# Threshold attention and an ELU layer on one core: two kinds of TensorE stretches of a pair joined, the tails' turned squares moved

## The chip, the cores and the metric

One core of a Trainium2 chip runs the kernel. The metric is the device time of one execution in microseconds (us), the median of several runs. TensorE is called PE, VectorE DVE, ScalarE ACT, GpSimd POOL; SP (SyncE) issues nearly all transfers.

## The reference

```python
# q, k, v: (8, 8, 576, 64) fp32; tau 0.02; w_in (512, 2048); w_out (2048, 512)
scores = scale * np.matmul(q, k.transpose(0, 1, 3, 2))
thresh = np.max(scores, axis=-1, keepdims=True) - tau
scores = np.where(scores >= thresh, scores, -1000000000.0)
scores = scores - np.max(scores, axis=-1, keepdims=True)
attn = np.exp(scores)
attn = attn / (np.sum(attn, axis=-1, keepdims=True) + 1e-09)
attn_out = np.matmul(attn, v)
x = attn_out.transpose(0, 2, 1, 3).reshape(8 * 576, 512)
h = x @ w_in
g = np.where(h > 0.0, h, np.exp(np.minimum(h, 0.0)) - 1.0)
out = g @ w_out
```

Per head, 576 queries meet 576 keys; a weight is kept where the score lies within tau of the row's maximum. The heads' outputs, put side by side, go through two dense layers with an ELU between. All of it is fp32.

## The kernel before, in words

**Work.** Heads are taken two at a time: 32 pairs (8 batches of 4 pairs). A head's 576 rows are four blocks of 128 (blocks 0 to 3) and a tail of 64; the two tails of a pair make block 4. Scores have the head's 64 dimensions as contraction, so they use 64 of the array's 128 rows: the two heads lie in the two row halves, and the output is cut into column halves of 64 too (tile form 64\*64, four quarters at once). Every other matmul contracts over 128 rows and is cut into column halves alone (128\*64).

**A step of the steady stage** (line numbers of the kernel before; pairs START = 9 to 31, the loop near line 1798) puts on PE, for pair p:
- `tail_step` (1725), which calls `tails_and_values` (829): scores of pair p's tails (line 852) and, beside them in the other quarters, the tails' part of the values of pair p − 2 (857), all 64\*64; then the main part of those values in 128\*64 (865, part 1 of 320 columns, then part 0 of 256);
- `wide_step` (1741) half 0: scores of blocks 0 and 1 (`wide_scores`, 785, matmuls on line 802);
- `ffn_quarters` (1692): 14 quarters of the dense layers' products (line 772, through `by_columns`). The products are Strassen-like (seven products for eight); they are fed by sums of blocks of x (`sums_x`, 1086), which are made once in four pairs;
- half 1: scores of blocks 2 and 3, and 14 more quarters.

**After the scores.** For each block and head: maximum (DVE, 809), bound (POOL, 818), exponential (ACT, 822), mask with sum (DVE, 826), then reciprocal (560) and scaling (POOL, 503). The weights of a block are turned with `turn_squares` (644): DVE transposes 32x32 squares into a buffer `x` of the pool `squares` (two buffers), SP sends it to DRAM in four transfers (683), and `fetch` (689) brings it back into its place in `wTa` (blocks 0 and 1) or `wTb` (blocks 2 and 3, three to four squares wide, with block 4's square fetched to the edges of both). These are what the values of the pair read in `tail_step` two steps later.

**PSUM.** Eight banks of 512 fp32 columns: five are the tile `sc` (the wide scores, and in its banks 1 to 4 values and the tails' scores), three are f0, f1, f2, which the products take in turn.

**What sets the order.** An agenda (`at`, 1432; `on_pe`, 1449) sorts all instructions by due times, which advance with PE's planned costs. `MOVED` shifts the due time of a named instruction in odd steps ("f...") or even steps ("s..."), `FIRST` in one step; names are like turn2 (the transposes of block 2) or fetch3. Each engine runs its own queue in that order and waits only for semaphores. SP's queue is in order too: a fetch that waits for its send holds what is behind it. The early stage (pairs 0 to 8) follows a hand-written list, `EARLY`. `on_banks` (744) adds the waits among engines bank by bank for the tile `sc`, in place of waits for the whole tile.

Of the kernel before, what the change touches and what calls it, by code (L numbers as in the profile page):

```python
# [20 lines left out]
    "9:3.0": 0.61, "9:fetch0": -3.6, "9:turn4": 2.44, "e:139.1": 0.46, "e:140.2": -0.49, "e:176.2": 1.07,  # L21
    "e:203p0": 1.03, "e:30.2": 0.35, "e:73p0": 1.88, "e:75p0": 1.3, "e:77.2": -1.81, "e:78.1": -3.94, "e:9b":
    -2.29, "e:e30": -0.75,
# [140 lines left out]
half.61 bsend.8.0 bmax.8.3.0 bmax.8.3.1 bmax.8.2.1 bth.8.3 half.58 bnorm.8.1.1 bmax.8.2.0 v.8 chg.7.0 bturn.8.1  # L164
bexp.8.2.0 bth.8.2 half.59 chg.1.1 bexp.8.2.1 scale.9 bexp.8.3.0 landed.7.4 bmask.8.2.1 fin.1.0 bmask.8.2.0 half.62
bsend.8.1 bexp.8.3.1 bsu.8.2 bmask.8.3.0 brec.8.2 half.63 bmask.8.3.1 bnorm.8.2.1 bnorm.8.2.0:act load.k.10 bsu.8.3
brec.8.3 bturn.8.2 bnorm.8.3.1 fin.1.1 bnorm.8.3.0 store.0.0 bturn.8.3 store.1.0 store.1.1 bsend.8.2 bsend.8.3
# [9 lines left out]
def kernel(  # L177
# [10 lines left out]
    nc = tc.nc  # L188
# [35 lines left out]
    granted, banks_at_start = [None], {x: psum["f"].tile([P, 512], FP32, name=x) for x in ("f0", "f1", "f2")}  # L224
# [233 lines left out]
    wTs, xts, open_steps, turns = {}, {}, {}, {}  # L458
# [230 lines left out]
    def fetch(pr, i, queue=nc.sync):  # L689
        back = turns.pop((pr, i)).rearrange("c k p n -> (c k) p n")  # L690
        wT, g0 = turned_tile(pr, i)
# [52 lines left out]
    def on_banks(made, ap, kept=True):  # L744

        ins, needed, starts = made.ins, [], [ap.offset % (5 * 512)]
# [19 lines left out]
        tc.add_to_no_dep_group(engine, ins)  # L766

    def by_columns(o, left, right, note=None, **how):
        n = o.shape[0]
        for y in range(0, n, D):  # L770
            oy = o[y : y + D] if n > D else o
            made = nc.tensor.matmul(oy, left[:, y : y + D] if n > D else left, right, skip_group_check=True, **how)  # L772
            if note:
                note(made, oy)

    def watch(made, ap):
        if ap.tensor.name == wide[0].tensor.name:
            on_banks(made, ap)
# [6 lines left out]
    def wide_scores(pr, half, parts=(0, 1)):  # L785

        qT, kT, _ = pairs[pr]
        for s in range(2) if parts[0] == 0 else ():
            i = 2 * half + s
            st = open_step(pr, i, turned_by[1 - s])  # L790
# [3 lines left out]
        order = (((0, 0, 0, 448), (1, 1, 0, 320), (1, 1, 320, 256), (0, 0, 448, 128)),  # L794
                 ((1, 0, 0, 256), (0, 1, 0, 384), (1, 0, 256, 320), (0, 1, 384, 192)))
        for h, s, c, n in [x for part in parts for x in order[part]]:
# [7 lines left out]
            if (h, s, c) == (1, 1, 0):  # L804
                on_banks(nc.scalar.copy(seen, o[:, :1]), o[:, :1], kept=False)

    def wide_max(pr, i, h):
        st = open_steps[pr, i]
        on_banks(nc.vector.tensor_reduce(st["mx"][:, h : h + 1], st["sc", h], axis=AX.XY if i == NC else AX.X, op=ALU.max,  # L809
# [19 lines left out]
    def tails_and_values(pr, before):  # L829

        pv, sc = (wide[0].rearrange("p (x n) -> p x n", n=512)[:, b : b + 2] for b in (1, 3))
# [15 lines left out]
        for a in range(2):  # L847
            for h in range(2):
# [5 lines left out]
                if before is not None:  # L854
                    g0, g1 = span(h, x)
                    o = pv[r, x, g0 * T : g1 * T]
# [1311 lines left out]
```

## Time and profile before

| | us |
|---|---|
| median of three runs | 1256.89 |
| lowest, highest | 1255.64, 1258.02 |
| profiled execution | 1254.87 |
| its span, first to last instruction | 1253.1 |
| DVE, POOL, ACT busy | 1067.1, 790.8, 585.1 |

The page of the profile gives the busy time of each engine, the granted clock, the chain of work that ended last, and groups of instructions by line. The views used beside it are the waits (who waited for whom), the timeline (instructions in order of time, merged by line) and windows (busy time of each engine in a stretch). A length of a matmul in the timeline has a modelled end; starts are recorded. A pair's step is about 33.9 us long.

### The profile page before, as it was taken

How to read it: one execution, taken by the hardware profiler on the slowest of the kernel's cores; microseconds unless marked ns; L12 is line 12 of the kernel's file. 1: busy time of each engine (PE TensorE's matmuls, PEld its weight loads, DVE VectorE, ACT ScalarE, POOL GpSimd, SP SyncE). 2: the span in 40 equal slices, each digit the busy share in tenths (PEclk: the TensorE clock that was granted, in tenths of full speed). 3: DMA queues.
4: the chain of work that ended last, by engine and by line, in shares of the span. 5: the costliest groups of instructions: out<-in, count | busy, mean ns of one | idle time of the engine just before them, and what ended most of it. 6: DMA issues, size and time to landing. Idle time of an engine off the chain costs nothing.

```text
span 1253.1 us, 32264 instructions
## 1 busy us (share of the span) xinstructions
PE 1238.7 (99%) x11999; PEld 826.4 (66%) x11999; DVE 1067.1 (85%) x2322; ACT 585.1 (47%) x1276; POOL 790.8 (63%) x1147
## 2 busy tenths in 40 slices
PE   8999999999999999999999999999999999999998
PEld 5776576466666666666666666666666666678887
DVE  6998989898889889898889888988989885777877
ACT  7987755453534445352625353444535260434130
POOL 5775545686576747674767657675767473675564
PEclk9999999999999999999999999999999999999999
DMA  8568899998989898899889898989889876444433
GB/s 226 151 181 240 231 256 262 251 293 222 267 204 261 230 244 223 260 251 244 236 228 269 224 261 211 266 222 249 215 258 251 238 217 223 163 139 153 137 112 116
DMA packets 332940, 278.31 MB, mean 222 GB/s; under 512 B 201328, under 2 KB 288368, under 8 KB 332784
## 3 DMA queue, kind: packets, MB, share of 16 engines
q1 hardware_dynamic: 331264, 275.57, 79.2%
q8 instruction: 94, 1.54, 0.5%
q10 hardware_dynamic: 1520, 0.69, 0.2%
q14 instruction: 62, 0.51, 0.1%
HBM read 178.85 MB, written 97.32 MB: 220 GB/s over the span
## 4 chain that ended last, share of the span: by engine, by line
PE 84%; DVE 1%; DMA 0%; issue 0%; ACT 0%; POOL 0%; SPq 0%; DVEq 0%; ACTq 0%; POOLq 0%
PE f L772 61%; PE sc L865 9%; PE sc L802 9%; PE f L992 2%; PE sc L857 1%; PE f L924 1%; PE sc L852 1%; DMA wTb<-there 0%; DVE mx L809 0%; DVE x L649 0%; DVE w_one L826 0%; DVE e L826 0%; DVE x L662 0%; DVE g L938 0%; ACT w_one L426 0%
## 5 line engine op out<-in xcount | busy, mean ns | idle before, releaser
L809 DVE TENSOR_REDUCE mx<-sc 128x1 f32<-128x576 f32 x252 | 180.1, 746 | 33.0 <-PE sc L802 28.6
L822 ACT ACTIVATE w_one<-sc,mx 128x576 f32<-128x576 f32 x140 | 100.9, 741 | 131.9 <-DVE mx L809 110.7
L818 POOL TENSOR_SCALAR th<-mx,ntau 128x2 f32<-128x2 f32 (+1 forms) x140 | 45.9, 329 | 183.1 <-DVE mx L809 183.0
L826 DVE SCALAR_TENSOR_TENSOR w_one<-sc,th,w_one 128x576 f32<-128x576 f32 x140 | 110.0, 813 | 20.3 <-ACT w_one L822 19.0
L772 PE MATMUL f<-xt,sw 128*64 128x256 f32 x1024 | 123.2, 382 | 0.6 <-ACT xt L432 0.5
L802 PE MATMUL sc<-kT,qT 64*64 64x320 f32 (+5 forms) x1792 | 122.2, 409 | 1.3 <-DVE su L554 0.5
L772 PE MATMUL f<-x,w_in_sb 128*64 128x256 f32 x1024 | 123.0, 380 | 0.0
L822 ACT ACTIVATE e<-sc,mx 128x576 f32<-128x576 f32 x112 | 82.9, 743 | 85.6 <-DVE mx L809 84.2
L772 PE MATMUL f<-xt,w_in_sb 128*64 128x256 f32 x1024 | 121.8, 379 | 0.5 <-DVE xt L1092 0.5
L503 POOL TENSOR_SCALAR w_one<-w_one,rs 128x576 f32<-128x576 f32 x115 | 89.4, 787 | 38.8 <-DVE rs L560 38.8
L649 DVE STREAM_TRANSPOSE x<-w_one 128x512 f32<-128x512 f32 (+1 forms) x140 | 100.0, 744 | 14.7 <-POOL w_one L503 9.6
L802 PEld LDWEIGHTS sc<-kT,qT 64*64 64x64 f32 x1792 | 81.1, 132 | 45.6 <-issue 18.5
L772 PE MATMUL f<-w_out_sb,s 128*64 128x256 f32 (+1 forms) x896 | 105.6, 376 | 0.0
L772 PE MATMUL f<-w_out_sb,g 128*64 128x256 f32 (+1 forms) x864 | 101.7, 376 | 0.0
L772 PEld LDWEIGHTS f<-x,w_in_sb 128*64 128x64 f32 x1024 | 74.4, 137 | 37.5 <-ACT g L1547 4.4
L772 PEld LDWEIGHTS f<-xt,w_in_sb 128*64 128x64 f32 x1024 | 75.4, 137 | 35.8 <-ACT e L822 0.9
L772 PEld LDWEIGHTS f<-xt,sw 128*64 128x64 f32 x1024 | 71.8, 137 | 40.9 <-issue 5.5
L826 DVE SCALAR_TENSOR_TENSOR e<-sc,th,e 128x576 f32<-128x576 f32 x112 | 87.8, 808 | 7.8 <-ACT e L822 7.4
L772 PE MATMUL f<-t,s 128*64 128x256 f32 (+1 forms) x800 | 93.5, 375 | 0.0
L772 PEld LDWEIGHTS f<-w_out_sb,s 128*64 128x64 f32 x896 | 63.7, 137 | 31.5 <-issue 3.2
L772 PEld LDWEIGHTS f<-w_out_sb,g 128*64 128x64 f32 x864 | 61.2, 137 | 31.7 <-issue 3.7
L649 DVE STREAM_TRANSPOSE x<-e 128x640 f32<-128x640 f32 x108 | 77.5, 756 | 3.6 <-POOL e L429 0.8
(324 smaller groups left out, 2800.5 us busy)
## 6 DMA issues: line engine op xcount, KB each, us to landing
there<-x SPq DMA_DIRECT2D x452, 144.0 KB, 3.9
wTb<-there SPq DMA_DIRECT2D x58, 576.0 KB, 6.5
wTa<-there SPq DMA_DIRECT2D x55, 576.0 KB, 4.9
sw<-win_sums SPq DMA_DIRECT2D x62, 384.0 KB, 4.1
t<-wout_sums SPq DMA_DIRECT2D x45, 512.0 KB, 5.3
there<-x SPq DMA_DIRECT2D x112, 80.0 KB, 1.9
wTb<-there SPq DMA_DIRECT2D x56, 160.0 KB, 3.7
wst<-in_moe_w_in_dram SPq DMA_DIRECT2D x16, 512.0 KB, 5.2
```

Of the source, the lines that this page charges most:

```text
L503: nc.gpsimd.tensor_scalar(wv, wv, st["rs"][:, h : h + 1], 1.0, ALU.mult, ALU.mult)
L649: nc.vector.transpose(x[:, :, c0 : c0 + nc_], src.rearrange("p (c g n) -> p g c n", c=nc_, n=T))
L772: made = nc.tensor.matmul(oy, left[:, y : y + D] if n > D else left, right, skip_group_check=True, **how)
L802: on_banks(nc.tensor.matmul(oy, qT[r, i * P + y * D : i * P + (y + 1) * D], kT[r, k0 : k0 + n], start=True, stop=True, skip_group_check=Tr ...
L809: on_banks(nc.vector.tensor_reduce(st["mx"][:, h : h + 1], st["sc", h], axis=AX.XY if i == NC else AX.X, op=ALU.max, negate=True), st["sc" ...
L818: nc.gpsimd.tensor_scalar(st["th"][:, cs], st["mx"][:, cs], -1.0, ntau, ALU.mult, ALU.add)
L822: on_banks(nc.scalar.activation(st["e", h], st["sc", h], AF.Exp, bias=st["mx"][:, h : h + 1]), st["sc", h])
L826: on_banks(nc.vector.scalar_tensor_tensor(st["e", h], st["sc", h], st["th"][:, h : h + 1], st["e", h], ALU.is_ge, ALU.mult, accum_out=st[" ...
L852: on_banks(nc.tensor.matmul(o, qT[r, MAIN:], kT[r, TAIL + x * HALF : TAIL + (x + 1) * HALF], start=True, stop=True, skip_group_check=True), o)
L857: on_banks(nc.tensor.matmul(o, vd[r, r], parts[x][r, g0:g1, NC], start=True, stop=False, skip_group_check=True), o)
L865: on_banks(nc.tensor.matmul(o, vm[:, h, c], parts[part][:, g0:g1, h * (NC + 1) + c], start=False, stop=(c == NC - 1), skip_group_check=Tru ...
L992: nc.tensor.matmul(cur[c, i][:, :DM], hidden(c, ft % NU, 1)[:, 0, ft // NU, i], w_out_sb[:, ft], start=(ft == 0), stop=(ft == NFT - 1))
```

## The change

The order of PE's work in a step is changed. `wide_step(pr - 1, 1)`, the scores of blocks 2 and 3 of the pair before, now stands directly ahead of `tail_step(pr)`, and the first 14 quarters directly behind the values; then come the scores of blocks 0 and 1 and the other 14 quarters. The tail step of the steady stage is the new `tails_apart`: the tails' scores lie behind the four wide ones, in the last columns of a tile `sc` that has six banks (f0 is its sixth), and the values lie in the product banks f2 (part 1) and f1 (part 0). After a tail step the products' banks come in the order f2, f0, f1.

With scores of blocks 2, 3 and 4 in hand at once there are three squares to turn; block 4's is now turned into the place in `wTb` that belongs to block 3 of the pair before and isn't fetched yet. The input sums are made in halves: the first half a pair earlier (for the first group in the early stage, on POOL by the list), the second around the tail step. Helpers tell the framework that groups of instructions use different banks. The due times, `FIRST` and `MOVED` are new for nearly all names. In the last stage six banks instead of five come from the closed tile, and the weights' sums of step 32 follow the last transposes.

```diff
@@ tables of due times (cut; two of the names that are spoken of)
-    1.44, "sturn1": 0.3, "sturn2": -0.07, "sturn3": 0.1, "sturn4": -3.1, "sx0": -0.87, "sx1": -0.05, "sx10":
+    7.54, "ssum4": 1.62, "sturn0": 2.13, "sturn1": 4.55, "sturn2": 7.64, "sturn3": 6.15, "sturn4": 5.52, "sw8": 0.32,
+    "fturn1": 4.12, "fturn2": 5.56, "fturn3": 5.24, "fturn4": 3.76, "fx0": 0.22, "fx1": -0.22, "fx10": 2.53, "fx11":
@@ PSUM
-    wide = [psum["w"].tile([P, 5 * 512], FP32, name="sc")]
-    banks_at_start["t"] = wide[0][:, 4 * 512 :]
+    wide = [psum["w"].tile([P, 6 * 512], FP32, name="sc")]
+    banks_at_start["f0"] = wide[0][:, 5 * 512 :]
+    banks_at_start["t"] = wide[0][:, 4 * 512 : 5 * 512]
@@ turn_squares
-        x = squares.tile([P, NT, NCH, T], FP32, name="x")
+        if i == NC and pr > START:
+            assert (pr - 1, 3) not in fetched
+            wT, g0 = turned_tile(pr - 1, 3)
+            x = wT[:, g0 : g0 + NT]
+        else:
+            x = squares.tile([P, NT, NCH, T], FP32, name="x")
@@ wide_scores
-            if (h, s, c) == (1, 1, 0):
+            if (h, s, c) == (1, 1, 0) or seen_too and (h, s, c) == (1, 0, 256):
                 on_banks(nc.scalar.copy(seen, o[:, :1]), o[:, :1], kept=False)
@@ new: the tail step of the steady stage
+    def tails_apart(pr, before):
+        places = [banks_at_start[x] for x in (("f2", "f1") if pr == START else ("f1", "f2"))] if before != NP - 1 else (wide[0][:, :512], wide[0][:, 512:1024])
+        sc = wide[0][:, 2 * T + 4 * S : 2 * T + 5 * S]
...
+        cut = 5 * 512 - 2 * T - 4 * S
+        for x, c, n in ((1, cut, S - cut), (0, 0, cut)):
+            for h in range(2):
+                r = slice(h * D, (h + 1) * D)
+                if before is not None:
+                    g0, g1 = span(h, x)
+                    o = places[x][r, g0 * T : g1 * T]
+                    watch(nc.tensor.matmul(o, vd[r, r], parts[x][r, g0:g1, NC], start=True, stop=False, skip_group_check=True), o)
+                if pr is not None:
+                    o = sc[D - h * D : P - h * D, c : c + n]
+                    on_banks(nc.tensor.matmul(o, qT[r, MAIN:], kT[r, TAIL + c : TAIL + c + n], start=True, stop=True,
+                                              skip_group_check=True), o)
@@ new: input sums by halves
+    def half_sums_x(g, rooms, j, engine=nc.vector):
+        (b11, b12), (b21, b22) = ([xts[g][:, k + j, t : t + CT] for t in (0, CT)] for k in (0, 2))
...
@@ tail_step
-                at(t + 3.3, lambda: wide_mask(pr, NC, 0), "mask4")
-                finish_of(pr, NC, t + 4.2, t + 10.5)
+                at(e + 3.0, lambda: wide_mask(pr, NC, 0), "mask4")
+                finish_of(pr, NC, e + 3.9, e + 5.4)
...
+            for x in ("f1", "f0", "f2") if pr == START else ("f2", "f0", "f1"):
+                ends.remove(banks_at_start[x])
+                ends.append(banks_at_start[x])
@@ wide_step (e: planned end of the scores)
-                finish_of(pr, i, e + (5.1, 7.8)[s], e + (8.4, 10.5)[s])
+                finish_of(pr, i, e + SUMS[half][s], e + TURNS[half][s])
+        BOUNDS, SUMS, TURNS = ((1.55, 3.05), (5.9, 0.9)), ((5.1, 7.8), (9.6, 3.6)), ((8.4, 10.5), (11.4, 9.4))
@@ the loop over pairs
-                for x, i in enumerate((NC, 0, 1, 2, 3)):
-                    at(t + 6.0 + 3.8 * x, lambda pr=pr, i=i: fetch(pr - 1, i), f"fetch{i}")
+                for i, when in ((NC, 9.0), (0, 12.5), (1, 16.0), (2, 20.0), (3, 24.0)):
+                    at(t + when, lambda pr=pr, i=i: fetch(pr - 1, i), f"fetch{i}")
+            if START < pr <= NP:
+                wide_step(pr - 1, 1)
             tail_step(pr)
...
-            for half in range(2):
-                if pr < NP:
-                    wide_step(pr, half)
...
-                ffn_quarters(HALF_QUARTERS)
+            next_q(pr)
+            ffn_quarters(HALF_QUARTERS)
+            if pr < NP:
+                e = clock[0] + 2.15
+                wide_step(pr, 0)
+                next_k(pr)
...
+                ffn_quarters(HALF_QUARTERS)
+            else:
+                extras(clock[0] + 0.6)
+                ffn_quarters(5)
+                while not all((NP - 1, i) in turns_done for i in range(NB)):
+                    do_next()
...
+                ffn_quarters(HALF_QUARTERS - 5)
@@ the last stage
+        ends.remove(banks_at_start["f0"])
         banks.close()
-        psum["f"] = ctx.enter_context(tc.tile_pool(name="ps_f3", bufs=5, space=PSUM))
+        psum["f"] = ctx.enter_context(tc.tile_pool(name="ps_f3", bufs=6, space=PSUM))
```

More of the change, by code (lines that the diff above doesn't have):

```diff
@@ L766, in on_banks @@
         tc.add_to_no_dep_group(engine, ins)
+        if (max(starts) + ap.ap[-1][1] - 1) // 512 < 5:
+            if apart:
+                other_banks(ins, "scores", "products")
+            else:
+                other_banks(ins, "values", "products", (nc.scalar, nc.vector))
+                other_banks(ins, "values", "outs")
     def by_columns(o, left, right, note=None, **how):
@@ L771, in by_columns, with watch, other_banks, beside @@
             oy = o[y : y + D] if n > D else o
[L772 to L776, printed above, removed]
+            (note or beside)(nc.tensor.matmul(oy, left[:, y : y + D] if n > D else left, right, skip_group_check=True, **how), oy)
+    def watch(made, ap, apart=True):
         if ap.tensor.name == wide[0].tensor.name:
-            on_banks(made, ap)
+            on_banks(made, ap, apart)
+    def other_banks(ins, mine, theirs, engines=(nc.tensor, nc.scalar, nc.vector)):
+        for e in engines:
+            if e.engine != ins.engine:
+                tc.declare_no_dep(ins, group=f"{theirs}{e.engine}", reason="other banks")
+        tc.add_to_no_dep_group(f"{mine}{ins.engine}", ins)
+    def beside(made, ap):
+        if ap.tensor.name == wide[0].tensor.name:
+            other_banks(made.ins, "products", "scores")
+            if made.ins.engine != nc.tensor.engine:
+                other_banks(made.ins, "products", "values", (nc.scalar, nc.vector))
+        return made
     def open_step(pr, i, w):
@@ L808, in wide_max @@
         st = open_steps[pr, i]
[L809 removed]
+        on_banks(nc.vector.tensor_reduce(st["mx"][:, h : h + 1], st["sc", h], axis=AX.XY if len(st["sc", h].shape) > 2 else AX.X, op=ALU.max,
                                          negate=True),
@@ new lines, in tails_apart, with span, values_main @@
+    def tails_apart(pr, before):
+        places = [banks_at_start[x] for x in (("f2", "f1") if pr == START else ("f1", "f2"))] if before != NP - 1 else (wide[0][:, :512], wide[0][:, 512:1024])
+        sc = wide[0][:, 2 * T + 4 * S : 2 * T + 5 * S]
+        if pr is not None:
+            qT, kT, _ = pairs[pr]
+            st = open_step(pr, NC, turned_by[0])
+            st["sc", 0], st["e", 0] = sc, st["w"][:, :S]
+        if before is not None:
+            b, j = divmod(before, NPAIR)
+            vm, vd = (raws[before][x] for x in ("vm", "vd"))
+            parts = [wTs.pop((before, part)) for part in range(2)]
+            if b not in xts:
+                xts[b] = xpool.tile([P, KJ, MAIN], FP32, name="xt")
+        def span(h, part):
+            return (2 * h, 2 * h + 10) if part else (0, 2 * NT)
+        cut = 5 * 512 - 2 * T - 4 * S
+        for x, c, n in ((1, cut, S - cut), (0, 0, cut)):
+            for h in range(2):
+                r = slice(h * D, (h + 1) * D)
+                if before is not None:
+                    g0, g1 = span(h, x)
+                    o = places[x][r, g0 * T : g1 * T]
+                    watch(nc.tensor.matmul(o, vd[r, r], parts[x][r, g0:g1, NC], start=True, stop=False, skip_group_check=True), o)
+                if pr is not None:
+                    o = sc[D - h * D : P - h * D, c : c + n]
+                    on_banks(nc.tensor.matmul(o, qT[r, MAIN:], kT[r, TAIL + c : TAIL + c + n], start=True, stop=True,
+                                              skip_group_check=True), o)
+        def values_main(part):
+            for c in range(NC):
+                for h in range(2):
+                    g0, g1 = span(h, part)
+                    o = places[part][h * D : (h + 1) * D, g0 * T : g1 * T]
+                    watch(nc.tensor.matmul(o, vm[:, h, c], parts[part][:, g0:g1, h * (NC + 1) + c], start=False,
+                                           stop=(c == NC - 1), skip_group_check=True), o)
+        return values_main, [lambda e="act", part=part: values_out(before, part, places[part], None, e) for part in range(2)]
@@ L991, in run @@
             for ft in range(4 * part + 2 * k, 4 * part + 2 * k + 2):
-                nc.tensor.matmul(cur[c, i][:, :DM], hidden(c, ft % NU, 1)[:, 0, ft // NU, i], w_out_sb[:, ft],
-                                 start=(ft == 0), stop=(ft == NFT - 1))
+                o = cur[c, i][:, :DM]
+                made = beside(nc.tensor.matmul(o, hidden(c, ft % NU, 1)[:, 0, ft // NU, i], w_out_sb[:, ft],
+                                               start=(ft == 0), stop=(ft == NFT - 1)), o)
+                if o.tensor.name == wide[0].tensor.name:
+                    other_banks(made.ins, "outs", "values")
         ot = []
@@ L1305, in early_tasks, with sum_x @@
             job(("insend", u), "sp|act", lambda e, u=(u + 2) % NU: send_in(u, engine_of[e]), ("in", u, 2))
+        def sum_x(m, engine):
+            if ("x", 1) not in in_sums:
+                in_sums["x", 1] = [late["x"].tile([P, 2, CT], FP32, name=f"x{x}") for x in range(3)]
+            half_sums_x(1, in_sums["x", 1], 0, engine)[m]()
+        for x, m in enumerate(X_ORDER):
+            job(("xe", m), "pool|dve", lambda e, m=m: sum_x(m, engine_of[e]), ("outv", START - 3, 0), ("outv", START - 3, 1), "late",
+                ("xe", X_ORDER[x - 1]) if x else None)
         last_w0 = [m for m in range(per_seq) if m % 3 == 2][-1]
@@ L1327, in early_tasks @@
                     job(("wsc", pr, half, y), "pe", lambda e, pr=pr, half=half, y=y: wide_scores(pr, half, (y,)),
-                        ("wsc", pr, half, 0) if y else ("tail", pr) if not half else ("wsc", pr, 0, 1), *ready_of[pr], *users,
+                        ("wsc", pr, half, 0) if y else ("tail", pr) if not half else ("wsc", pr, 0, 1), *ready_of[pr],
+                        *[x for x in users if y or x[0] != "outv" or x[2]],
                         soft=() if y else steps_b[-4] + steps_b[-3])
```

170 lines of the change are left out of this document (98 added, 72 removed), and 76 rows, old and new, of tables (FIRST, MOVED).

## The prediction

> **What bounds the kernel now.** I read the page first (busy shares, clock, chain), then the PE waits, then PE's timeline over one whole step.
>
> ```profile
> span 1253.1 us, 32264 instructions
> PE 1238.7 (99%) x11999; PEld 826.4 (66%) x11999; DVE 1067.1 (85%) x2322; ACT 585.1 (47%) x1276; POOL 790.8 (63%) x1147
> PEclk9999999999999999999999999999999999999999
> PE 84%; DVE 1%; DMA 0%; issue 0%; ACT 0%; POOL 0%; SPq 0%; DVEq 0%; ACTq 0%; POOLq 0%
> ```
>
> TensorE is busy for 99% of the span, its clock is never throttled, and the chain that ended last is TensorE's own for 84%. So the time moves only if TensorE's stream gets shorter, or if something makes it wait. In the steady stage it hardly waits; these are the longest waits there:
>
> ```profile
> PE f L772 <- DVE xt L1092: 0.5, 1, 0.5
> PE sc L802 <- DVE su L554: 0.5, 1, 0.5
> PE f L772 <- ACT xt L432: 0.5, 1, 0.5
> PE sc L772 <- DMA wTb<-there: 0.2, 1, 0.2
> ```
>
> What is left is inside "busy". The timeline of one even step (pair 20, with the start of its second scores at the end) shows it. Columns: start, length, line, tile form, shape, count.
>
> ```profile
> 605.24 2.17 PE L802 MATMUL sc<-kT,qT 64*64 64x448 f32 x32
> 607.34 1.95 PE L772 MATMUL f<-xt,sw 128*64 128x256 f32 x16
> ...
> 620.01 0.45 PE L852 MATMUL sc<-kT,qT 64*64 64x288 f32 x1
> ...
> 620.03 0.48 PE L857 MATMUL sc<-wTb,vd 64*64 64x320 f32 x1
> ...
> 620.35 0.58 PE L857 MATMUL sc<-wTb,vd 64*64 64x320 f32 x2
> ...
> 620.76 0.43 PE L857 MATMUL sc<-wTb,vd 64*64 64x320 f32 x1
> ...
> 621.14 2.37 PE L865 MATMUL sc<-wTb,vm 128*64 128x320 f32 x16
> ...
> 625.17 2.17 PE L802 MATMUL sc<-kT,qT 64*64 64x448 f32 x32
> 627.27 1.95 PE L772 MATMUL f<-w_out_sb,g 128*64 128x256 f32 x16
> 629.05 1.90 PE L772 MATMUL f<-t,g 128*64 128x256 f32 x16
> ...
> 637.68 1.90 PE L772 MATMUL f<-t,s 128*64 128x256 f32 x16
> 639.51 0.97 PE L802 MATMUL sc<-kT,qT 64*64 64x448 f32 x8
> ```
>
> Lengths include a modelled end, so I use starts. The array changes its tile form six times a step: tails (64\*64), values (128\*64), scores (64\*64), 14 quarters of products (128\*64), scores, products. Each stretch has a fixed cost:
> - 64\*64: the tails stream 1152 columns through each quarter of the array (each fp32 matmul runs twice, so scores 2×2×288, values' tails 2×(256+320)) in 621.14 − 620.01 = 1.13. A half of the scores streams 2304 in 607.34 − 605.24 = 2.10. Twice 1.13 less 2.10 leaves **0.16** that does not grow with the work; 1152 columns cost 0.97.
> - 128\*64: inside a stretch 16 rows take (637.68 − 629.05)/5 = 1.726. The seven groups from 627.27 to 639.51 take 12.24, less 7 × 1.726 = 12.08: again **0.16**.
>
> A check from the last pairs, where no scores interrupt:
>
> ```profile
> 1028.41 2.38 PE L865 MATMUL sc<-wTb,vm 128*64 128x320 f32 x16
> ...
> 1056.61 0.43 PE L857 MATMUL sc<-wTa,vd 64*64 64x256 f32 x1
> ```
>
> Values and 28 quarters in one stretch take 28.20. In pieces they take 4.03 (625.17 − 621.14) + 2 × 12.24 = 28.51. Two stretches fewer, 0.31 less.
>
> **The change, part by part.**
>
> *Order on TensorE.* A step becomes: second scores of the pair before, then the tails; values, then 14 quarters; first scores; 14 quarters. The built order has the same 6131 matmuls and 1368 SP transfers, and does put scores and tails, and values and products, back to back. That is four stretches for six in pairs 9 to 31: 23 × (0.16 + 0.16) = **−7.4 us**. The step falls from 33.84 to 33.52. All of it is on the path.
>
> *The tails' two heads.* Before, values' tails of one column part went to a bank of their own per head at a time; now both heads write one bank (f2, then f1) from the two row halves, as do both heads' scores. Row L857, 64x320, bears on that: its four passes are the two heads' writes into the same bank. The second of head 1 starts at 620.35 and streams 0.27 (320 of 1152 columns that cost 0.97), and the group's other, head 0's first, starts at 620.35 + 0.58 − 0.43 = 620.50. So they overlap by 0.12, while the stage keeps its 1.13. I take 0; the other end is a rival below.
>
> *DVE and ACT.* The only added work: 35 input sums of 512 columns become 70 of 256 (65 DVE, 5 POOL), and 23 "seen" copies.
>
> ```profile
> L1090 DVE TENSOR_TENSOR x<-xt 128x512 f32<-128x512 f32 x14 | 9.5, 679 | 2.1 <-ACT xt L432 2.1
> L1508 DVE TENSOR_TENSOR g<-f,t 128x256 f32<-128x256 f32 x56 | 23.6, 422 | 8.8 <-POOL t L1505 7.3 <-POOL kT L432 0.3
> L1505 POOL TENSOR_TENSOR u<-u,w 128x256 f32<-128x256 f32 x64 | 54.4, 850 | 23.3 <-ACT u L1500 14.8 <-DVE x L1789 8.6
> L805 ACT COPY seen<-sc 128x1 f32<-128x1 f32 x56 | 8.9, 159 | 66.0 <-PE sc L802 66.0
> 585.74:620.01 34.27, 34.17 (x339) 21.41 (x337) 29.31 (x65) 19.23 (x44) 20.56 (x32) 1.00 0.85 246
> 653.84:687.79 33.95, 33.95 (x339) 21.45 (x337) 32.10 (x70) 19.20 (x44) 22.29 (x32) 1.00 0.96 275
> ```
>
> 65 × 0.42 − 35 × 0.68 = 3.5 us of DVE over 23 steps (0, if a half costs half, to 65 × 0.68 − 23.8 = 20). DVE (third busy figure of the window rows) has 2 to 5 us free in a step, ACT 15: hidden. Without that cover it would be 3.5. At pair 9 the DVE-fed wait of 0.52 goes, but five sums at up to 0.85 (4.3 in all) enter POOL's queue ahead of the first product: −0.5 to +4.3 once, I take 0, as half of them have half a step's lead.
>
> *Banks.* Values now lie in f2 and f1 and the tails' scores partly in f0, so the first products queue behind their readers.
>
> ```profile
> 623.53 0.74 ACT L822 ACTIVATE w_one<-sc,mx 128x576 f32<-128x576 f32 x1 [0.33 <-DVE mx L809]
> 624.17 0.36 ACT L432 COPY xt<-sc 128x256 f32<-128x256 f32 x1
> 624.42 0.43 ACT L432 COPY xs<-sc 64x64 f32<-64x64 f32 x2
> ```
>
> The first product needs f2, whose three copies (about 0.7 us) start when part 1 ends; part 0 runs 1.83 longer. Margin 1.1, or 0.4 with an exponential of 0.74 in front: 0. f0 must be released by the tails' mask (due 3 us after them), f0's product begins 4.9 after: 0. Behind a late ACT stand the product copies, for which TensorE waits a bank later.
>
> *The turned weights' way.* Here the slack goes. Blocks 2 and 3 are scored at a step's start instead of mid-step before, yet values want them at the same place. Their chain: transposes on DVE, four sends on SP, landing, fetch on SP, landing.
>
> ```profile
> 581.99 1.44 DVE L649 STREAM_TRANSPOSE x<-e 128x640 f32<-128x640 f32 x2
> 583.45 2.26 SPq L683 DMA_DIRECT2D there<-x  x4
> 638.33 1.94 SPq L683 DMA_DIRECT2D there<-x  x4
> 641.15 3.58 SPq L683 DMA_DIRECT2D there<-x  x4
> there<-x SPq DMA_DIRECT2D x452, 144.0 KB, 3.9
> wTb<-there SPq DMA_DIRECT2D x58, 576.0 KB, 6.5
> ```
>
> The due times hold on the chip: before, pair 18's block 2 is due at 581.8 (scores' end 573.5 + 8.4 − 0.07) and runs at 581.99. After, in even steps, it is due 19.04 after scores' end, t + 21.2 from the step's start t. Add 1.44 + 2.0 of sends (their last starts near t + 24.1) and 3.9: t + 28.0. The fetches follow, block 3's 0.5 later: landed at t + 35.0. Values want them at t + 33.52 + 1.94 (scores now stand ahead) = t + 35.5. Margin **0.5**; in odd steps, due 2.1 earlier, 2.6. SP holds the next sends and loads behind such a fetch. When the sends take 3.58 for 1.94, an even step is 1.64 later: a wait of 1.1. So 0 to 11 × 1.1 = 12 us over the 11 even steps; I take **+1.5**, near the usual row (1.94 to 2.26). The tails' square in the fourth step's place of wTb needs values' part 1 read (t + 5.3) and is due after t + 12: 0, and it keeps a third square from waiting for two buffers.
>
> *Ends.* In step 32 no scores stand ahead of the last values, so t + 35.0 would meet a need at t + 31.6: 3.4 late, were that chain not freed by tails, first scores and preparations that are missing there. 0 to 3.4; I take 0.
>
> **Sum:** 1254.87 (profiled run; 1.8 outside its span) − 7.4 + 1.5 = 1249.0. The median shown, 1256.89, is 2.0 above the profiled run, so I forecast **1251.0**.
>
> **The rivals.**
> - *Fetches late (slower).* If even steps end 1.64 late in sends and another 1.1 in landings, each waits 2.2: 11 × 2.2 = 24, −7.4 = +16.8, so 1273.7; with the sends alone +4.6, so 1261.5. It decides from 7.4/11 = 0.67 of wait, that is, when the chain is 1.2 longer than by medians. For it: margin 0.5, SP's rows of 3.58, DMA shares up to 0.96. Against: odd steps have room, and medians just fit.
> - *Bank handover (no change).* The copies of f2 come 0.3 late in each pair (two exponentials ahead): 23 × 0.3 = 6.9, so 1257.9. Against: margin 0.4 with one ahead.
> - *Row halves cannot share a bank (slower).* The tails' 0.97 would double: 23 × 0.97 = 22.3, so 1273.3. The overlap of 0.12 in row L857 speaks against it. The Trainium skill states it as a rule: TensorEngine Tiling (Array Packing), Gotcha 1: PSUM Pressure, says that different row tiles cannot access the same PSUM bank at the same time. By that rule the change loses; the trace does not agree for halves that write different partitions.
> - *More than forecast.* No new wait, and the old ones (0.5, 0.5 and smaller) gone: 1247.5 or a little under.
> - *No merging:* excluded by the built order, but for a fixed cost that is tied to something else: 1%, 1257.
>
> **How the numbers follow.** Forecast 0.63 (its own range 1247.5 to 1254), more 0.07, fetches late 0.14, handover 0.11, shared bank 0.04, no merging 0.01. A measurement tells about 0.2% (2.5 us) from no change. Faster 0.63 + 0.07 = 0.70; within 0.2% 0.11 + 0.01 = 0.12; slower 0.14 + 0.04 = 0.18. The range runs from 1246.5 (all old waits gone, spread of runs) to 1262, the late sends' price; what lies beyond holds about 2 in 10.
>
> **What would show it.** Right: 64\*64 stretches of 3.07 (2.10 + 0.97), 128\*64 stretches of about 16.1 from values' start to the first scores, steps of 33.5. Fetches: a wait at values' tails named "DMA wTb<-there", in odd steps (after even ones). Handover: a wait of the first product for ACT's xs or DVE's mask. Shared bank: scores and tails of 4 rather than 3.07. Wrong altogether: stretches merged, yet steps of 33.8 without a wait.

## The result, and the profile after

| | before | after |
|---|---|---|
| median, us | 1256.59 | 1274.85 (1269.77 to 1281.75) |
| profiled execution, us | 1254.87 | 1277.47 |
| its span, us | 1253.1 | 1275.7 |

The ratio is 1.0144 (95% interval 1.011 to 1.0178): 18.3 us slower, where 5.9 us faster was forecast. The page of the profile after, its lines for the span, TensorE, the chain that ended last, and two kinds of transfers with their median time to landing:

```profile
span 1275.7 us, 32318 instructions
PE 1237.7 (97%) x11999; PEld 832.8 (65%) x11999; DVE 1066.9 (84%) x2352; ACT 586.7 (46%) x1299; POOL 800.4 (63%) x1152
...
PE 80%; DMA 10%; DVE 4%; SPq 2%; ACT 1%; issue 1%; POOL 1%; DVEq 0%; POOLq 0%; ACTq 0%
...
there<-x SPq DMA_DIRECT2D x452, 144.0 KB, 3.9
wTb<-there SPq DMA_DIRECT2D x58, 576.0 KB, 5.2
```

TensorE's busy time is nearly the old one; the span is 22.6 longer. The chain, which held 0% of DMA before, now holds 10%, and 2% of SP's queue. These two kinds of transfer are no slower than before (3.9 and 6.5 then); the fetch into wTa is (5.6, 4.9 then).

**What was gained is there.** TensorE's timeline of an undisturbed step after (columns: start, length, line, tile form, shape, count):

```profile
906.26 0.43 PE L947 MATMUL f<-wTb,vd 64*64 64x320 f32 x1
...
907.34 2.37 PE L958 MATMUL f<-wTb,vm 128*64 128x320 f32 x16
...
923.46 2.17 PE L851 MATMUL sc<-kT,qT 64*64 64x448 f32 x32
...
937.80 2.17 PE L851 MATMUL sc<-kT,qT 64*64 64x448 f32 x32
939.79 0.43 PE L947 MATMUL f<-wTb,vd 64*64 64x320 f32 x1
...
940.87 1.56 PE L958 MATMUL f<-wTb,vm 128*64 128x320 f32 x9
```

Read the starts. Second scores and tails last 940.87 − 937.80 = 3.07 (forecast 3.07), values with 14 quarters 923.46 − 907.34 = 16.12 (16.1), the whole step 939.79 − 906.26 = 33.53 (33.52).

**What was lost are waits.** TensorE's largest waits after (total, times, longest):

```profile
PE f L947 <- DMA wTb<-there: 11.3, 5, 3.6
PE sc L809 <- DVE su L579: 3.6, 4, 1.3
PE sc L851 <- DVE w_one L875: 3.2, 4, 1.4
PE sc L947 <- DMA there_w<-w_one: 2.5, 1, 2.5
PE f L947 <- DMA sw<-win_sums: 2.1, 1, 2.1
```

Line 947 is the values' tails. The third row lies in the early stage (120.67 to 210.06, and it is in stale_fetch below as well, 2.8), the fourth row is the last values, in step 32; the others lie in the steady stage. The fourth and the fifth row name other transfers than wTb's fetch, but in both places the second fetch lands just before TensorE goes on: issued at 1072.09 it took 6.65, TensorE went on at 1078.98; issued at 757.58 it took 6.61, TensorE went on at 764.44. So I take all seven waits of line 947 as waits for turned weights. By the starts of the values' tails, the steps of pairs 11, 13, 17, 21, 23, 25 and 29 are 1.3 to 5.1 us longer than 33.53, all of them odd. Of the even steps, 24 is 0.9 longer; 26 and 30, each right behind a long wait, are 1.7 longer without one (the last section says why).

And the busy times of 800 us of the steady stage (TensorE's is the second figure), first before, then after:

```profile
245.00:1045.00 800.00, 799.38 (x7889) 507.56 (x7889) 693.41 (x1523) 351.33 (x770) 524.23 (x784) 1.00 0.88 241
```

```profile
245.00:1045.00 800.00, 780.25 (x7702) 501.67 (x7700) 680.42 (x1521) 347.33 (x779) 518.23 (x767) 0.99 0.86 236
```

TensorE stood still for 0.6 us in it before, and for 19.8 after (800 less its busy time). The DMA engines are not busier (0.88, then 0.86).

**One late step (pair 29), followed back.** First DVE's transposes of blocks 3 and 2, then SP's queue, then the chain that ended last in this stretch, all of the kernel after:

```profile
953.20 1.44 DVE L679 STREAM_TRANSPOSE x<-e 128x640 f32<-128x640 f32 x2
954.76 1.44 DVE L679 STREAM_TRANSPOSE x<-w_one 128x640 f32<-128x640 f32 x2
...
962.98 0.78 DVE L465 STREAM_TRANSPOSE kT<-qm 128x576 f32<-128x576 f32 x1 [1.17 <-DMA qm<-in_k_dram]
```

```profile
949.95 0.54 SPq L378 DMA_DIRECT2D vm<-in_v_dram  x1
...
955.07 1.93 SPq L698 DMA_DIRECT2D there<-wTb  x4
957.04 3.52 SPq L364 DMA_DIRECT2D qm<-in_k_dram  x4
...
961.67 5.02 SPq L713 DMA_DIRECT2D there<-x  x8
969.47 1.91 SPq L724 DMA_DIRECT2D wTb<-there  x2
```

```profile
961.14 5.23 DMA wTa<-there
...
966.39 4.58 DMA there<-x
...
971.04 7.08 DMA wTb<-there
...
978.37 0.54 PE f L947
```

Both squares are turned by 956.2, on time. SP reaches their sends at 961.67: it is still issuing v loads, the tails' square and k loads. The eight sends take 5.02, since the last one waits until the fetch issued eight transfers before it (961.14) has landed. SP then stands until 969.47 for the first fetch's sends, and until 970.97 for the second's, whose last one lands then. The second fetch lands at 978.12, and the values' tails begin at 978.37; this is the longest of the five waits above, 3.6. Meanwhile DVE waits for a k load that SP issued late (the 1.17 in the last of DVE's rows).

SP's own waits say the same of the whole run. First before (the fetch was line 693), then after:

```profile
SPq L693 <- DMA there<-x: 2.8, 4, 1.2
```

```profile
SPq L724 <- DMA there<-x: 64.1, 58, 4.3
...
SPq L713 <- DMA t<-wout_sums: 12.2, 14, 1.9
```

Before, the sends of blocks 2 and 3 had more than half a step to land before they were fetched. Block 2 of pair 18 was sent from 583.45 on (a row in the prediction), and its fetch was this one:

```profile
606.41 0.45 SPq L693 DMA_DIRECT2D wTb<-there  x1
```

Now the fetch follows its send directly, and SP, an in-order queue, stands for 64.1 us, or 2.8 a step over 23 steps. A send has nothing to do with the loads of `t`; the third of SP's waits shows how a transfer waits for one that is several places ahead.

### The profile page after: what moved, and what is told of

Same layout as the page of the kernel before. It is cut to its first block, busy times and chain, and to the rows that moved or that the text cites. A ratio compares the mean times of both kernels' runs of the same rounds, so it can differ in the third digit from the quotient of the medians.

```text
span 1275.7 us, 32318 instructions
## 1 busy us (share of the span) xinstructions
PE 1237.7 (97%) x11999; PEld 832.8 (65%) x11999; DVE 1066.9 (84%) x2352; ACT 586.7 (46%) x1299; POOL 800.4 (63%) x1152
## 4 chain that ended last, share of the span: by engine, by line
PE 80%; DMA 10%; DVE 4%; SPq 2%; ACT 1%; issue 1%; POOL 1%; DVEq 0%; POOLq 0%; ACTq 0%
PE f L809 41%; PE sc L809 12%; PE f L958 8%; PE sc L851 7%; DMA there<-x 3%; DMA wTb<-there 3%; DMA wTa<-there 2%; PE f L1086 2%; PE f L947 2%; PE sc L520 2%; PE f L1045 1%; PE sc L1086 1%; SPq L713 1%; PE sc L588 1%; DVE mx L858 1%
## 5 line engine op out<-in xcount | busy, mean ns | idle before, releaser
L875 DVE SCALAR_TENSOR_TENSOR w_one<-sc,th,w_one 128x576 f32<-128x576 f32 x140 | 111.2, 809 | 18.3 <-ACT w_one L871 17.5
L851 PE MATMUL sc<-kT,qT 64*64 64x256 f32 (+5 forms) x1792 | 121.6, 409 | 3.2 <-DVE w_one L875 3.2
L528 POOL TENSOR_SCALAR w_one<-w_one,rs 128x576 f32<-128x576 f32 x115 | 92.0, 807 | 22.6 <-DVE rs L585 22.6
L809 PE MATMUL f<-x,w_in_sb 128*64 128x256 f32 x832 | 100.9, 379 | 0.0
L528 POOL TENSOR_SCALAR e<-e,rs 128x576 f32<-128x576 f32 x92 | 68.5, 747 | 42.4 <-DVE rs L585 41.0
L809 PE MATMUL f<-xt,sw 128*64 128x256 f32 x736 | 91.3, 381 | 0.7 <-ACT xt L457 0.5
L679 DVE STREAM_TRANSPOSE x<-w_one 128x640 f32<-128x640 f32 (+1 forms) x118 | 84.0, 748 | 8.6 <-POOL w_one L528 3.7
L809 PE MATMUL f<-xt,w_in_sb 128*64 128x256 f32 x736 | 90.9, 380 | 0.0
L854 ACT COPY seen<-sc 128x1 f32<-128x1 f32 x79 | 12.6, 159 | 157.7 <-PE sc L851 157.7
L809 PEld LDWEIGHTS f<-x,w_in_sb 128*64 128x64 f32 x832 | 61.6, 137 | 28.2
L809 PEld LDWEIGHTS f<-t,s 128*64 128x64 f32 x800 | 57.1, 137 | 28.1
L809 PEld LDWEIGHTS f<-xt,sw 128*64 128x64 f32 x736 | 53.4, 137 | 27.8 <-issue 3.7
```

Of the source, the lines that this page charges most:

```text
L528: nc.gpsimd.tensor_scalar(wv, wv, st["rs"][:, h : h + 1], 1.0, ALU.mult, ALU.mult)
L679: nc.vector.transpose(x[:, :, c0 : c0 + nc_], src.rearrange("p (c g n) -> p g c n", c=nc_, n=T))
L809: (note or beside)(nc.tensor.matmul(oy, left[:, y : y + D] if n > D else left, right, skip_group_check=True, **how), oy)
L851: on_banks(nc.tensor.matmul(oy, qT[r, i * P + y * D : i * P + (y + 1) * D], kT[r, k0 : k0 + n], start=True, stop=True, skip_group_check=Tr ...
L875: on_banks(nc.vector.scalar_tensor_tensor(st["e", h], st["sc", h], st["th"][:, h : h + 1], st["e", h], ALU.is_ge, ALU.mult, accum_out=st[" ...
```

## The experiments

Theory **Q**: SP's in-order queue. The fetch of blocks 2 and 3 waits there for its own fresh send and holds what is behind it; the queue, already behind in odd steps, then makes sends, fetches and k loads late. Rival **B**: the 16 DMA engines are the limit and any order is as late. Smaller rivals are named at their runs. Ratios are to the kernel before, run beside each (medians 1257.1 to 1258.2). A difference between two runs of the table is good to some 2 to 5 us, by their intervals. In stale_fetch, hold_only and two_more_issues the fetches read older squares, so these kernels leave out part of the reference's work; they only price the wait.

| run | median, us | ratio (95%) |
|---|---|---|
| stale_fetch | 1250.73 | 0.9944 (0.9929 to 0.9959) |
| hold_only | 1273.22 | 1.0127 (1.0105 to 1.0148) |
| two_more_issues | 1257.42 | 1.0001 (0.9982 to 1.0021) |
| square_back | 1282.44 | 1.0193 (1.0171 to 1.0216) |
| loads_act | 1318.70 | 1.0487 (1.0462 to 1.0511) |
| pool_fetch | 1371.70 | 1.0907 (1.0877 to 1.0936) |
| v_late | 1264.55 | 1.0056 (1.0029 to 1.0083) |
| v_k_late | 1266.81 | 1.0088 (1.0056 to 1.0119) |
| v_k_mid | 1255.09 | 0.9985 (0.9973 to 0.9997) |
| k_early | 1254.15 | 0.9982 (0.9964 to 1.0000) |
| k_early_w | 1255.34 | 0.9983 (0.9967 to 0.9998) |
| k_turn_after_add | 1254.99 | 0.9980 (0.9967 to 0.9992) |
| last_turns | 1257.73 | 1.0000 (0.9990 to 1.0011) |

### stale_fetch: the fetch without its fresh send

```diff
     def fetch(pr, i, queue=nc.sync):
-        back = turns.pop((pr, i)).rearrange("c k p n -> (c k) p n")
+        back = turns.pop((pr, i))
+        if pr >= START and i in (2, 3):
+            older[pr, i] = back
+            back = older.get((pr - 1, i), back)
+        back = back.rearrange("c k p n -> (c k) p n")
```

> The changed kernel (1274.9 us; 1256.6 before), with one edit: the fetch of turned blocks 2 and 3 reads the square that the pair before sent, so that it needs no send of its own step (the last column block's values are then those of other weights). Bytes, issues and their order stay. Theory Q (SP's in-order issue queue: such a fetch waits about 2.8 us a step there for its own fresh send to land, and holds all that is queued behind it; 58 waits, 64.1 us): the fetch's waits on SP fall from 64 to under 10 us, the fetch lands before the values' tails ask for it, and most of the 32 us of TensorE's waits go: 1249 to 1258 us. Theory B (the 16 DMA engines, busy 0.87 of the steady stage, are the limit, whatever the order): the landing times stay above 5 us and the time stays at 1268 to 1276.

Its waits, SP's fetch (line 730 here) and TensorE's values' tails (953):

```profile
SPq L730 <- DMA there<-x: 5.5, 6, 2.8
```

```profile
PE f L953 <- DMA wTb<-there: 1.3, 1, 1.3
```

The fetch's wait on SP falls from 64.1 to 5.5, that of TensorE from 11.3 to 1.3, and the time to 1250.73: 24.1 below the changed kernel and 7.0 below the one before. The traffic and its order are the same, and its page gives 5.9 us for a single fetch into wTb to land (5.2 in the changed kernel) at a busy share of the DMA engines of 0.88 in the same 800 us. So B as the cause is refuted: with the same bytes, and a fetch no faster, the waits are all but gone. And the joined stretches are worth what was forecast, 7 us, once TensorE hardly waits.

### hold_only and two_more_issues: which half of the wait harms

hold_only puts SP's wait back, behind fetches that are already issued; two_more_issues keeps the added copies and takes their wait away.

```diff
+            if (pr, 5 - i) in older and pr >= START and i in (2, 3):
+                for m in (2, 3):
+                    queue.dma_start(held[:, m], older[pr, m][:, 0, :, :1])   # hold_only
+                    queue.dma_start(held[:, m], older.get((pr - 1, m), older[pr, m])[:, 0, :, :1])   # two_more_issues
```

> The kernel stale_fetch (1250.7 us: blocks 2 and 3 fetched from the pair before), plus, behind the later of these two fetches, two tiny copies in DRAM that read four by four single numbers of this step's own squares of blocks 2 and 3: SP must wait there until the fresh sends have landed, as in the changed kernel, but the fetches themselves are already issued. This tells the two halves of the loss apart. If the loss is the fetch's own lateness: 1250 to 1254 us. If it is what SP holds back behind the wait (sw, q and k loads, then DVE's turns and the products): 1260 to 1272, with TensorE's waits named for DVE or for sw.

> As hold_only (1273.2 us), but the two tiny copies read the squares of the pair before, so SP waits for nothing there; what is left of hold_only's loss is then its two more issues (0.64 us each) a step. If the wait for the fresh sends is what costs: 1250 to 1256 us (stale_fetch without the copies: 1250.7). If SP's queue is so full that 1.3 us of issuing a step do the same harm as the wait: 1265 or more.

Waits of hold_only: SP's at the copies (734), then TensorE's largest, at the products (819).

```profile
SPq L734 <- DMA there<-x: 35.7, 36, 3.2
```

```profile
PE sc L819 <- DVE w_one L885: 7.3, 6, 2.4
```

And DVE's own, for a q load:

```profile
DVE qT L446 <- DMA qm<-in_q_dram: 13.8, 8, 3.3
```

hold_only is 22.5 above stale_fetch although the fetches themselves, which read older squares, are issued ahead of the wait: TensorE now waits mostly for DVE, and DVE for loads. So it is enough to hold the queue; who is late behind it changes with the order. The copies alone cost 1257.42 − 1250.73 = 6.7, a little more than the 5.3 at most that I had expected, and the wait 15.8. That two more issues a step (1.3 us) already cost 6.7 shows how little room SP's queue has; whether they harm by their issue time, or because later transfers must wait for them too, this run doesn't tell.

### square_back: the tails' square in the pool again

```diff
-        if i == NC and pr > START:
+        if False:
```

> The changed kernel with one part undone: the tails' turned square is again a third square of the two-buffer pool, not the idle fourth step of the turned weights. Theory Q: the place of this square has nothing to do with the waits; nothing gained, 1273 to 1285 (slower where the third square must wait for a buffer). Rival S (the square lies in wTb, so that wTb's fetches wait for its sends): the waits at the values' tails go, 1250 to 1260.

Waits of DVE, then of TensorE:

```profile
DVE x L679 <- DMA there<-x: 50.7, 13, 7.2
```

```profile
PE f L809 <- DVE g L1622: 14.1, 7, 3.5
```

By the medians 7.6 slower than the changed kernel, by the ratios 6 (1.0193 against 1.0144; the intervals just overlap). DVE, in order too, stands with a transpose until a buffer's sends have landed, and the adds behind it come late. TensorE's waits at the values' tails of the steady stage did go, as rival S says, but TensorE is late by DVE now, and SP still stands 60.2 us before the fetches. What refutes S is stale_fetch: there the square lies in wTb as well, and the waits are gone. The square's new place rather saves time.

### loads_act and pool_fetch: the same work from another queue

```diff
-                    at(e + 6.1, lambda: load(pr + 1, ("km",), True), "loadk")
+                    at(e + 6.1, lambda: load(pr + 1, ("km",), True, nc.scalar), "loadk")
```

(loads_act, the q and v loads likewise; pool_fetch gives `nc.gpsimd` to `fetch` for blocks 2 and 3.)

> The changed kernel with the q, k and v loads of the steady stage issued by ACT instead of SP (12 of some 36 issues a step); same bytes, same transfers. Theory Q: SP reaches the sends of blocks 3 and 2 in odd steps 3 to 5 us sooner, k loads no longer come late to DVE, and TensorE's waits at the values' tails (11 us and more) and in the second products go: 1250 to 1260 us. Theory B: no gain, 1270 to 1278. A third outcome: ACT is held by a load that waits for its buffer, and products wait for ACT's copies: waits of TensorE named for ACT, over 1275.

> The changed kernel with the fetches of blocks 2 and 3 issued by POOL instead of SP; same bytes, same waits for fresh sends, but now POOL is what stands still until they land. Theory Q (the harm is what SP holds back behind the wait): SP's 64 us of fetch waits go, k, q and sw loads come in time; POOL is free for 37% of the span and takes the wait, or passes it to DVE and the products where sums queue behind it: 1252 to 1268 us. If the fetch's own lateness is the harm: 1270 or more.

loads_act: SP's waits, ACT's, TensorE's.

```profile
SPq L1180 <- DMA qm<-in_q_dram: 33.7, 5, 8.1
```

```profile
ACT w_one L871 <- DMA qm<-in_k_dram: 22.4, 10, 4.1
```

```profile
PE f L809 <- ACT s L1614: 9.5, 14, 1.3
```

pool_fetch: POOL's waits, and DVE's.

```profile
POOL wTb L724 <- DMA there<-x: 122.4, 31, 9.0
```

```profile
DVE e L875 <- POOL th L867: 95.5, 22, 6.9
```

Both missed theory Q's range. In loads_act the third outcome came, much larger than written: ACT's exponentials stand behind loads that wait, and SP gets no freer, since its transfers now wait for loads that ACT issued. In pool_fetch the wait went to POOL (122.4 us), the bounds of the masks queue behind it, and DVE waits for those. My 1252 to 1268 was wrong; that the harm is in what stands behind the wait holds on POOL as on SP. The time over 1270 doesn't speak for the fetch's own lateness either: TensorE's largest waits there are for DVE (43.2 and 34.6 us), not for wTb. Nor is all of the loss waiting: the granted clock of its profiled run is 0.968 (0.996 in the changed kernel), which over a span of 1367 us makes some 40 us at most, an estimate. The Trainium skill says (Trainium Kernel Development and Optimization, Key Constraints) that transfers issued from SP, ACT and POOL run on the same 16 DMA engines, so that several issuers save only issue time. Here not even that was gained: ACT took over 12 issues a step, SP waited for them in its own transfers, and the time rose by 43.9.

### v_late, v_k_late, v_k_mid, k_early, k_early_w: the order on SP

| run (edits to the changed kernel) | v loads due (was t + 9) | k loads, odd steps | turn of k, odd steps |
|---|---|---|---|
| v_late | t + 27 | unchanged | unchanged |
| v_k_late | t + 27 | 3.8 later | 3.4 later |
| v_k_mid | t + 27 | 1.6 later, between the sends of blocks 3 and 2 | 4.4 later |
| k_early | t + 27 | 6.2 sooner (even steps 4.1) | unchanged |

k_early_w is k_early with the stores of step 32 due 4 us later.

```diff
-                at(t + 9.0, lambda pr=pr: load(pr, ("v",)))
+                at(t + 27.0, lambda pr=pr: load(pr, ("v",)))
-"floadk": 2.18, "floadq": -0.15, "fprep1": -3.43, "fkcopy": -0.2
+"floadk": 3.8, "floadq": 0.6, "fprep1": 1.0, "fkcopy": 1.5
```

(The second part is that of v_k_mid.)

> The changed kernel with the four v loads of a step asked for at 27 us into the step (behind the fetches) instead of 9 us. Same issues and bytes. Theory Q: four issues of 0.57 us go from ahead of the sends, which are 2.3 us sooner in odd steps; of the waits at the values' tails (0.4 to 4.9 us) about half goes, with some of the late k loads: 1260 to 1268 us. Theory B: within 3 us of 1274.9.

> The changed kernel with correct data and SP's order changed: v loads at 27 us into the step (as in v_late, 1264.5 us) and, in odd steps, the k loads behind the sends of blocks 3 and 2 (due 3.8 us later; the k turn that needs them 3.4 us later). Theory Q: the sends of odd steps leave 2 us sooner than in v_late, and the landing time that the fetch waits for is filled with the k loads; the remaining waits at the values' tails (odd steps, 1 to 4 us) go: 1250 to 1257 us. If the k loads, now later, hold DVE's turn of k: waits of the second products for DVE, 1260 or more. Theory B: no better than v_late.

> As v_k_late (1266.8 us; no wait at the values' tails is left, but 12 us of TensorE's waits in the second products of odd steps for DVE, which waits for k loads), with the k loads of odd steps between the sends of block 3 and block 2 (2.2 us sooner) and the turn of k 1 us later. Theory Q: the waits for DVE go, those at the values' tails stay away: 1250 to 1258 us. Theory B: both kinds of wait only trade places, about 1265.

> The changed kernel with v loads at 27 us as in v_late, and the k loads 4 to 6 us sooner in every step, at the place where the v loads were (the q turn that frees their buffer is due 3 us before). Now nothing but the tails' square and two loads stands ahead of the sends of blocks 3 and 2. Theory Q: both kinds of wait go: 1249 to 1256 us. Theory B (the DMA engines set the landing, whatever the order): 1264 as v_late.

> As k_early, and the 14 stores of changed output weights in step 32 are due 4 us later, so that they are not issued ahead of the last fetches (the last values' products wait 2.5 us there in the changed kernel). Expected 1.5 to 3 us less than k_early, if the last stage does not need those stores sooner; otherwise up to 4 more.

SP's wait at the fetch in v_late; then v_k_late, TensorE's and DVE's largest waits; then v_k_mid, SP's wait at the fetch:

```profile
SPq L724 <- DMA there<-x: 61.1, 65, 3.2
```

```profile
PE sc L809 <- DVE su L579: 12.2, 9, 3.3
```

```profile
DVE kT L465 <- DMA qm<-in_k_dram: 15.3, 9, 3.7
```

```profile
SPq L724 <- DMA there<-x: 51.8, 45, 2.9
```

v_late wins back 10.3 us with the fetch's wait hardly shorter: four issues fewer ahead of the sends are enough for that. It came as forecast; v_k_late missed theory Q's range and is the other case that its text names; v_k_mid and k_early lie in theory Q's ranges. In v_k_late no wait is left at the values' tails of the steady stage, but the k loads came too late for DVE, and the products wait for DVE. v_k_mid, with the k loads between, has neither in its profiled run (1250.48, the fastest of ten; the median is 1255.09), though SP still stands 51.8 us before fetches there. So the wait as such costs little where the queue has room; what is behind it, and how soon it is needed, decides. k_early comes to the same time by the other way. k_early_w brought no gain: the stores were not what made the last fetch late, for the last values still waited 2.8 us there (2.9 in k_early).

### k_turn_after_add and last_turns: two leftovers

v_k_mid leaves odd steps at 33.89. Its DVE rows there:

```profile
676.54 0.78 DVE L465 STREAM_TRANSPOSE kT<-qm 128x576 f32<-128x576 f32 x1
677.25 0.39 DVE L1622 TENSOR_TENSOR g<-f,s 128x256 f32<-128x256 f32 x1
```

The turn of k stands ahead of an add that frees a bank, and a product starts at 677.69, when the add has ended.

```diff
-"fprep1": 1.0, "fkcopy": 1.5, "floadq": 0.6
+"fprep1": 1.7, "fkcopy": 2.2, "floadq": 1.3   (both runs)
+"32:norm20": -1.7, "32:turn2": -1.5, "32:turn3": -1.5, "32:fetch2": -1.5, "32:fetch3": -1.5   (last_turns)
```

> As v_k_mid (1255.1 us, its profiled run 1250.5), with the turn of k in odd steps 0.7 us later, so that DVE does one add of the products (f with s) first: in v_k_mid a product waits 0.36 us in each of the 11 odd steps for the bank that this add reads. Expected: odd steps of 33.53 instead of 33.89, 4 us less: 1249 to 1253 us. If that small wait is not DVE's order: no change.

> As k_turn_after_add, and in step 32 alone the turns and fetches of the last blocks 3 and 2 are due 1.5 us sooner (the last values' tails and first products wait 2.1 us there for a fetch that lands at +31.1 us of the step). Expected: another 1 to 2 us less than k_turn_after_add, 1248 to 1252 us.

In k_turn_after_add undisturbed odd steps are 33.53 as expected, but the median stayed at 1254.99, above the 1249 to 1253 that was expected (runs from 1251.43 to 1258.54): in some steps the second fetch still lands late (in its profiled run at +35.9 us of pair 29's step, where +33.5 is needed), the margin being thin. Of the versions that leave nothing out it has the lowest ratio, 0.998, 2.5 us below the kernel before; v_k_mid and k_early can't be told from it. last_turns missed: nothing gained, by the median 2.7 lost, and in its profiled run, the slowest of twelve, the last values wait 4.0 us, more than in the runs above. Why the last fetch comes late stays open, and so does what spreads the landings from step to step.

## Why the prediction was wrong

- **What bounds the kernel, and the six stretches made four: right.** −7.4 forecast; 33.53 a step, and −7.0 in stale_fetch. The Trainium skill's rule weighed there (TensorEngine Tiling (Array Packing), Gotcha 1: PSUM Pressure) would have doubled the tails' part: the joined stretch is 3.07, so the trace does not agree with it for two heads in one bank, where they write different partitions.
- **DVE, ACT and banks: right.** No large wait named the bank handover or the added sums (ACT's xt 0.5 us once); stale_fetch, which has all of them, runs at the forecast.
- **The tails' square at 0: right in sign.** It keeps DVE from waiting for a buffer, as was said; square_back puts 6 to 8 us on that.
- **The turned weights' way: this step failed.** Its chain added DVE's due time, 1.44 of transposes, 2.0 of sends and landings by their medians, and so held that SP would reach the sends when DVE was done. DVE was on time, SP was not: 5.5 us late at pair 29. It left SP's place in the queue out of the sum: the 18 issues ahead of those sends, due within 7 us, took 11.7 at pair 29 (949.95 to 961.67), with transfers that wait for those eight places ahead, and the fetch's own wait of 2.8 a step, which the sentence "SP holds the next sends and loads behind such a fetch" named but didn't price. From the end of the transposes to the landing of the fetch the chain has 12.4 (t + 22.64 to t + 35.0); at pair 29 this took 21.9 (956.20 to 978.12). Of the 9.5 more, 5.5 are SP's coming late and 3.3 the sends, eight in a row, the last of which waits for the transfer eight places ahead (4.7 from first to last start, for 1.5 in the sum). So the margin of 2.6 in odd steps was none, and the waits came from odd steps, not even ones. +1.5 was taken; stale_fetch puts 24.1 on it, some 5 of that through TensorE's clock (last section), which the sum doesn't have at all.
- **The ends at 0:** the bound of 3.4 held, the value did not; the last values waited 2.5.
- **The rival and the chances.** The rival "fetches late" ended at 1273.7, near the result, and its sign of recognition, a wait at the values' tails named DMA wTb<-there, came. That the number is so near is luck: it counts 2.2 us in each of the 11 even steps, where seven odd steps, the end and the clock made the loss. It had 0.14. A margin of 0.5 us from medians, on a queue whose rows ran from 1.94 to 3.58 for the same sends, deserved a larger chance.

## What to carry to other kernels

When a change shortens the time between a send and the fetch that reads it back, price the fetch's wait as time of the queue that issues it, and ask what is queued behind it and when that is needed; a median landing time says nothing about when the queue gets to the transfer. Before moving transfers to another engine's queue, try their order: here taking v loads from ahead of the sends won back 10 us, where ACT and POOL as issuers lost 44 and 97. To learn whether a dependency or the traffic is at fault, let the reader fetch older data: bytes and order stay, the wait goes.

## What was not expected of the hardware

A wait of TensorE can cost more than its length. Two steps of the kernel after, the values' tails with their wait and the main part of the values behind them:

```profile
423.46 0.45 PE L947 MATMUL f<-wTb,vd 64*64 64x320 f32 x1 [2.77 <-DMA wTb<-there]
...
424.60 2.37 PE L958 MATMUL f<-wTb,vm 128*64 128x320 f32 x16
```

```profile
837.47 0.45 PE L947 MATMUL f<-wTb,vd 64*64 64x320 f32 x1 [2.95 <-DMA wTb<-there]
...
838.60 4.06 PE L958 MATMUL f<-wTb,vm 128*64 128x320 f32 x16
```

After 2.77 us the values took 2.37 as ever; after 2.95 they took 4.06, 1.7 more. The window of the second has a granted clock of 0.79 (the last figure but two; the DMA share stands behind it). Two more windows have the same clock, behind the wait of 3.65 at 978.37 and behind a much shorter one, 1.92 at 343.24:

```profile
837.00:845.00 8.00, 7.53 (x56) 4.37 (x58) 3.45 (x6) 2.25 (x6) 3.98 (x5) 0.79 0.79 216
978.00:986.00 8.00, 7.63 (x58) 4.44 (x60) 3.59 (x6) 2.31 (x6) 3.99 (x5) 0.79 0.78 201
343.00:351.00 8.00, 7.76 (x58) 4.75 (x62) 5.09 (x15) 3.90 (x9) 6.83 (x11) 0.79 0.95 237
```

```profile
343.24 1.55 PE L809 MATMUL sc<-xt,sw 128*64 128x256 f32 x8 [1.92 <-DVE g L1622]
```

Each costs 8 × (1 − 0.79) = 1.7 us: some 5 us of this run's loss are not waits but products and values at a lower clock. That is why the steps of pairs 26 and 30 are 1.7 longer. The length of the wait alone doesn't decide it: 1.92 and 2.95 were enough, 2.10 (at 764.44) and 2.77 were not.

The Trainium skill (TensorE: Matmul & The Clock Gate, Part 1: The HAM clock gate (the "warmup" mystery)) says that the clock is halved after an idle window of about 3.4 us and released after a busy one. The trace agrees in kind (a granted clock of 0.50 from 840 to 842), but not in the length as it is put here: waits of 1.92 and 2.95 us, both below 3.4, were enough.
